# The last output tile in three column parts, and the third w1 chunk in one load

## The chip, the cores and the metric

The kernel runs on one core of one Trainium2 chip. The metric is the device time in microseconds (us), as a median over runs. One profiled run of a kernel also leaves a trace; the span of a trace, from the first to the last instruction, is about 1.7 us shorter than the run's device time. For a program on one core a run counts as fast unless it is over 1.5% above the fastest run of the same kernel. The profile of the kernel before was taken in a throttled execution.

## The reference

Two branches on x (2048 rows, 512 columns, bf16) are mixed by a gate:

```python
g = sigmoid((x * gate_w).sum(-1, keepdims=True))
a = linear_attention(x, wqkv) @ wo         # 32 heads of 16, phi(t) = where(t>0, t+1, exp(t)) + 1e-6
h = layernorm(x)
u = gelu(einsum("bsd,sf->bdf", h, w1) + b1)                     # token MLP, F = 1792
b = (einsum("bdf,fs->bds", u, w2) + b2).transpose(0, 2, 1)
return g * a + (1 - g) * b
```

The change touches how w1 (2048 x 1792) is loaded and how the last 128 of the 2048 output rows are finished.

## The kernel before

w1 comes in four chunks: three of 512 columns (2 MB each) and one of 256 (1 MB). Chunks 0 to 2 are loaded in two halves, the last in one load. All are issued by SyncE's queue without waiting for a buffer, since there are four buffers.

```python
    for c, (j0, nb) in enumerate(w1_chunks):
        w = wpool.tile([P, NT, FB * P], BF16, name="w1c", tag="wc")
        w1c.append(w)
        for t0 in range(0, NT, 8) if c < 3 else (0,):
            t1 = t0 + 8 if c < 3 else NT
            nc.sync.dma_start(
                out=w[:, t0:t1, : nb * P], in_=w1_view[:, t0:t1, j0 * P : (j0 + nb) * P]
            )
        # ... after chunk 0: the loads of wv and wo
```

The output is made in 16 row tiles of 128 rows. Each takes 4 matmuls for the attention branch (`aps`) and 14 for the MLP (`yps`). VectorE mixes both into `ot` (the eviction), and a store follows. The last tile is already split: 384 columns with a store, then 128 columns with a store, so that the eviction of the wide piece runs behind the matmuls of the narrow one.

```python
    for t in range(NT):
        # ... aps: 4 matmuls of 512 columns; ScalarE makes a_sc from it
        for c0, W in ((0, D - P), (D - P, P)) if t == NT - 1 else ((0, D),):
            cs = slice(c0, c0 + W)
            yps = bank("yps")
            for f in range(NF):
                mm(yps[:, :W], w2c[c][:, f, tl * P : (tl + 1) * P], uT[:, f, cs], f == 0, f == NF - 1)
            ot = opool.tile([P, D], BF16, name="ot", tag="ot")
            nc.vector.scalar_tensor_tensor(
                out=ot[:, :W], in0=yps[:, :W], scalar=c1[:, t : t + 1], in1=a_sc[:, cs],
                op0=ALU.mult, op1=ALU.add,
            )
            (nc.scalar if t < 2 else nc.sync).dma_start(out=o_view[:, t, cs], in_=ot[:, :W])
        # ...
```

One thing is not in this source: the framework under it gives every transfer on the hardware queues one of eight completion counters (semaphore lanes), in rotation: the issues count on 100, 103, 104, 105, 106, 108, 109 and 110 in turn. In the instruction listing the loads of x and w1 wait for the transfer eight before them, on the same counter.

## Time and profile before

| | kernel before |
|---|---|
| time, median of the first 3 runs | 163.35 us (163.27 to 163.65) |
| profiled run | 281.43 us, span 279.7 us, granted TensorE clock 0.565: throttled |
| PE busy | 99% of the span |
| one late row tile, throttled | 6.94 us for 18 matmuls of 512 columns |

The first fence is from the page of the kernel before: busy time of each engine, the rows for granted clock and DMA in 40 slices of the span (tenths, then GB/s), and the chain of work that ended last.

```profile
span 279.7 us, 2222 instructions
...
PE 275.8 (99%) x826; PEld 97.0 (35%) x826; DVE 128.3 (46%) x273; ACT 73.8 (26%) x114; POOL 7.2 (3%) x17
...
PEclk9555555555555555555555555555555555555555
DMA  7999995000000008003400707000000000000000
GB/s 196 238 293 352 349 345 145 0 0 0 2 1 0 0 0 265 0 0 104 158 4 0 262 12 251 19 20 23 23 26 20 20 19 19 21 19 19 19 19 19
...
PE 97%; DMA 1%; SPq 0%; DVE 0%; issue 0%
...
```

PE is never free: the chain is 97% PE. The clock row reads 5 (tenths) nearly everywhere, so every PE duration here must be scaled before it says anything about the timed runs (386 ns per matmul of 512 columns here). DMA is busy in the first seven slices, then only in bursts for w2 and lightly for the stores.

The second fence is the timeline of the last tile (start, duration, engine, line, operation, count; in brackets the idle time before it and what ended it).

```profile
...
start us, us, engine line op out<-in xcount [idle before <-releaser]
...
271.45 5.51 PE L110 MATMUL yps<-uT,w2c 128*128 128x384 bf16 x28
...
275.48 1.21 PEld L110 LDWEIGHTS <-w2c 128*128 128x128 bf16 x13 [0.15 <-issue]
275.73 0.62 DVE L500 SCALAR_TENSOR_TENSOR ot<-yps,c,a_sc 128x384 bf16<-128x384 f32 x1 [4.79 <-PE yps L110]
276.99 0.35 DVE L500 SCALAR_TENSOR_TENSOR ot<-yps,c,a_sc 128x128 bf16<-128x128 f32 x1 [0.64 <-PE yps L110]
```

The 28 matmuls of both pieces are merged into one row. The 384-column eviction is done (275.73 + 0.62 us) before the last matmuls end, so the last eviction (276.99) waits for PE alone. The thirteen last weight loads take 1.21 us, 93 ns each: about the pace of 128 columns at this clock (386/4 = 96 ns). The w1 loads are seven issues, the last begun at 34.5 us:

```profile
...
L173 SPq DMA_DIRECT2D w1c<-in_B_w_dram x7: 507/2914/4284, 16.8 to 34.5; - x7
...
```

### The profile page before, as it was taken

The numbers are of one execution on the slowest core, as the hardware profiler recorded it, in microseconds if no ns is written. First come the engines' busy times: TensorE is split into PE (matmuls) and PEld (weight loads), VectorE is DVE, ScalarE is ACT, GpSimd is POOL, SyncE is SP. The second block draws the span as 40 slices with busy tenths as digits, with TensorE's granted clock in tenths as the row PEclk, the third lists the DMA queues.
The fourth block names the chain that finished last, engine by engine and source line by source line (L and its number), as shares of the span: only waits on it lengthen the run. The fifth ranks groups of instructions, "written<-read, shape, count | busy, mean of one in ns | idle before, by whom it ended". The sixth has DMA issues, their size and how long they took to land.

```text
span 279.7 us, 2222 instructions
## 1 busy us (share of the span) xinstructions
PE 275.8 (99%) x826; PEld 97.0 (35%) x826; DVE 128.3 (46%) x273; ACT 73.8 (26%) x114; POOL 7.2 (3%) x17
## 2 busy tenths in 40 slices
PE   8999999999999999999999999999999999999996
PEld 3333333333333333333333333333333333333333
DVE  1835566256465571256597701565555553111111
ACT  3411344124434160235511211222222221111110
POOL 1000310010100000000000000000000000000000
PEclk9555555555555555555555555555555555555555
DMA  7999995000000008003400707000000000000000
GB/s 196 238 293 352 349 345 145 0 0 0 2 1 0 0 0 265 0 0 104 158 4 0 262 12 251 19 20 23 23 26 20 20 19 19 21 19 19 19 19 19
DMA packets 29241, 22.94 MB, mean 82 GB/s; under 512 B 7696, under 2 KB 29200, under 8 KB 29232
## 3 DMA queue, kind: packets, MB, share of 16 engines
q1 hardware_dynamic: 28288, 21.89, 26.2%
q10 hardware_dynamic: 832, 0.79, 0.8%
q0 software_dynamic: 112, 0.14, 0.2%
q8 instruction: 6, 0.10, 0.1%
q14 instruction: 3, 0.02, 0.0%
HBM read 19.01 MB, written 2.10 MB: 75 GB/s over the span
## 4 chain that ended last, share of the span: by engine, by line
PE 97%; DMA 1%; SPq 0%; DVE 0%; issue 0%
PE uacc L110 31%; PE yps L110 31%; PE kacc L110 9%; PE aps L110 9%; PE qacc L110 9%; PE gacc L110 9%; DMA xs<-in_A_x_dram 1%; PE pt L110 0%; PE kvps L110 0%; PE w2ps L110 0%; SPq L126 0%; DVE ot L500 0%; PE pt L327 0%
## 5 line engine op out<-in xcount | busy, mean ns | idle before, releaser
L110 PE MATMUL uacc<-hs,w1c 128*128 128x512 bf16 (+1 forms) x233 | 89.6, 581 | 0.0
L110 PE MATMUL yps<-uT,w2c 128*128 128x512 bf16 (+2 forms) x238 | 89.3, 560 | 0.0
L110 PEld LDWEIGHTS <-w2c 128*128 128x128 bf16 x238 | 31.2, 133 | 55.5 <-issue 55.4
L110 PEld LDWEIGHTS <-w1c 128*128 128x128 bf16 (+1 forms) x233 | 29.4, 131 | 55.3 <-issue 55.2
L500 DVE SCALAR_TENSOR_TENSOR ot<-yps,c,a_sc 128x512 bf16<-128x512 f32 (+2 forms) x17 | 12.2, 719 | 68.6 <-PE yps L110 68.6
L487 ACT ACTIVATE a_sc<-aps,c,gg 128x512 f32<-128x512 f32 x16 | 12.4, 775 | 76.0 <-PE aps L110 76.0
L110 PE MATMUL aps<-W2sb,pqT 128*128 128x512 bf16 x64 | 27.8, 582 | 0.0
L110 PE MATMUL qacc<-xT,wq_sb 128*128 128x512 bf16 x64 | 27.7, 581 | 0.0
L110 PE MATMUL kacc<-wk_sb,xT 128*128 128x512 bf16 x64 | 27.4, 589 | 0.0
L110 PE MATMUL gacc<-pk,xs 128*128 128x512 bf16 x64 | 26.8, 579 | 0.0
L211 DVE TENSOR_SCALAR e<-e 128x512 bf16<-128x512 bf16 x32 | 9.4, 293 | 34.2 <-ACT e L210 34.2
L321 ACT ACTIVATE uT<-uacc,bcol 128x512 bf16<-128x512 f32 x14 | 9.4, 686 | 46.8 <-PE uacc L110 46.8
L386 DVE STREAM_TRANSPOSE zT<-pz 128x512 f32<-128x512 f32 x16 | 11.3, 706 | 18.3 <-ACT pz L385 18.3
L210 ACT ACTIVATE e<-qacc 128x512 bf16<-128x512 f32 x16 | 9.6, 597 | 27.6 <-PE qacc L110 27.6
L210 ACT ACTIVATE e<-kacc 128x512 bf16<-128x512 f32 x16 | 9.6, 597 | 26.7 <-PE kacc L110 26.7
L110 PEld LDWEIGHTS <-xs 128*128 128x128 bf16 x76 | 9.8, 133 | 17.8 <-issue 16.3
L385 ACT ACTIVATE pz<-pqT,zcol 128x512 f32<-128x512 bf16 x16 | 11.4, 714 | 11.5 <-DVE ot L500 11.4
L110 PEld LDWEIGHTS <-wq_sb 128*128 128x128 bf16 x64 | 8.6, 135 | 16.0 <-issue 16.0
L110 PEld LDWEIGHTS <-pqT 128*128 128x128 bf16 x64 | 8.4, 132 | 16.0 <-issue 16.0
L110 PEld LDWEIGHTS <-xT 128*128 128x128 bf16 x64 | 8.2, 130 | 15.3 <-issue 14.7
L250 ACT ACTIVATE hs<-xs,nmr,rstd 128x512 bf16<-128x512 bf16 x16 | 12.7, 802 | 0.0
L395 DVE STREAM_TRANSPOSE rex<-rd 128x512 bf16<-128x512 bf16 x16 | 11.4, 711 | 0.6
(59 smaller groups left out, 116.3 us busy)
## 6 DMA issues: line engine op xcount, KB each, us to landing
w1c<-in_B_w_dram SPq DMA_DIRECT2D x7, 1024.0 KB, 12.4
w2c<-in_B_w_dram SPq DMA_DIRECT2D x8, 896.0 KB, 5.7
out_dram<-ot SPq DMA_DIRECT2D x13, 128.0 KB, 1.7
xs<-in_A_x_dram SPq DMA_DIRECT2D x3, 512.0 KB, 4.4
xs<-in_A_x_dram SPq DMA_DIRECT2D x4, 128.0 KB, 3.3
wk_sb<-in_A_wqkv_dram ACTq DMA_DIRECT2D x2, 256.0 KB, 3.3
wq_sb<-in_A_wqkv_dram SPq DMA_DIRECT2D x1, 512.0 KB, 4.8
wv_sb<-in_A_wqkv_dram SPq DMA_DIRECT2D x1, 512.0 KB, 10.0
```

The lines of the kernel that those rows point to most:

```text
L110: nc.tensor.matmul(o, lhsT=lhsT, rhs=rhs, start=start, stop=stop, **kw)
L210: nc.scalar.activation(out=e[:], in_=acc[:], func=ACT.Exp)
L211: nc.vector.tensor_scalar(out=e[:], in0=e[:], scalar1=1.0, scalar2=PHI_EPS, op0=ALU.min, op1=ALU.add)
L250: nc.scalar.activation(out=hs[:, t, :], in_=xs[:, t, :], func=ACT.Identity, scale=rstd[:, t : t + 1], bias=nmr[:, t : t + 1],)
L321: nc.scalar.activation(out=uT[:, j, :], in_=acc[:], func=ACT.Gelu_apprx_tanh, bias=bcol[:, j : j + 1])
L385: nc.scalar.activation(out=pz[:], in_=seg, func=ACT.Copy, scale=zcol[:, j : j + 1])
L386: nc.vector.transpose(out=zT[:], in_=pz[:])
L395: nc.vector.transpose(out=rex[:].rearrange("p (a d) -> p a d", d=HEAD), in_=rd[:].unsqueeze(2).to_broadcast([P, SC // HEAD, HEAD]),)
L487: nc.scalar.activation(out=a_sc[:], in_=aps[:], func=ACT.Identity, scale=gg[:, t : t + 1], bias=c2[:, t : t + 1],)
L500: nc.vector.scalar_tensor_tensor(out=ot[:, :W], in0=yps[:, :W], scalar=c1[:, t : t + 1], in1=a_sc[:, cs], op0=ALU.mult, op1=ALU.add,)
```

## The change

The last tile in three parts of 256, 128 and 128 columns, and the third w1 chunk in one load. The apparent intent is to have less work left when the matmuls end, and one transfer less.

```diff
-        for t0 in range(0, NT, 8) if c < 3 else (0,):
-            t1 = t0 + 8 if c < 3 else NT
+        for t0 in range(0, NT, 8) if c < 2 else (0,):
+            t1 = t0 + 8 if c < 2 else NT
...
-        for c0, W in ((0, D - P), (D - P, P)) if t == NT - 1 else ((0, D),):
+        for c0, W in ((0, 2 * P), (2 * P, P), (3 * P, P)) if t == NT - 1 else ((0, D),):
```

## The prediction

> **What bounds the kernel.** The page shows PE busy 99% of the span, and the chain of waits is 97% PE matmuls; DMA is 1% of it. The profile fell in a throttled execution: span 279.7 us at a granted clock of 0.565, while the timed runs took 163.35 us, so I scale it. In the timeline a late row tile (4 aps and 14 yps matmuls of 512 columns) takes 6.94 us, 386 ns per matmul. [...] with 6.9 us of start, 2.7 us of tail, and 1.7 us by which the profiled run's time exceeds its span, 162.3 us. About 1 us is left for stalls of fast runs alone. So fast runs too are bound by matmul columns.
>
> **The w1 load.** One 2 MB load replaces two of 1 MB. In the profile all w1 transfers are issued by 37.7 us, and the DMA row is empty after the seventh slice (49 us). [...] Chunk 0, needed first, lies ahead in the same queue and isn't touched. One load less shifts the semaphore lanes of later transfers and gives w2 loads waits on lanes long done. Worth on the critical path: 0.0 us.
>
> **The last tile.** Before: 14 matmuls of 384 columns, then 14 of 128. After: 256, 128, 128. PE columns are equal; 14 weight loads and matmuls are added. In the trace the last 13 weight loads run 93 ns apart, which is 128 columns at 0.57 of full clock: narrow matmuls still pay only for columns. [...] The last piece stays 128 columns: its eviction (0.35 us) and store (1.4 us to landing) are unchanged.
>
> Was the last piece held up by the 384 piece? At full clock (T = end of the 384 matmuls): eviction T+0.05 to 0.67, store issue 0.70 to 1.03 (0.62 and 0.33 us in the trace); the last matmul ends at T+0.78, its eviction runs to 1.15, its store issues at 1.20. Neither DVE nor the queue is late, by 0.1 to 0.2 us. The split relieves only a near miss: the store ahead of the last one shrinks from 96 to 32 KB and sits 0.78 us, not 0.5 us, ahead. I allow 0 to 0.15 us for less overlap of the transfers. Net: -0.05 us, +-0.1.
>
> **Prediction.** 163.3 us, range 162.9 to 163.75. Faster by over 2%: 1%; within 2%: 97%; slower by over 2%: 2%.
>
> **What would show it.** At equal clock: 840 instead of 826 PE matmuls; the PE stretches before the last tile unchanged; no PE wait on w1c; 18 evictions at the output line, 17 before; the last eviction starting within 0.05 us of the last matmul, the last store landing in 1.4 us. The stretch from the last aps matmul to the end within 0.2 us of before.
>
> **What would make it wrong.** A throttled state in the timed runs (the profile shows that it exists), narrow matmuls bound at full clock by weight load (over 60 ns each), the middle store's issue delaying the last, or a stall in fast runs at w1 that the throttled profile hides and that the shifted lanes move.

In the first paragraph the sum of 162.3 us has lost the PE stretch scaled to full clock, 151 us. It can be had from what was measured afterwards: in the trace of the changed kernel 15 late row tiles, 270 matmuls, take 58.275 us, 215.8 ns each, and 270.1 x 215.8/386 = 151 us. In the second an estimate of when chunk 2 is first read is cut; measured, it is 31.8 us after the chunk landed. In the third a fixed cost for the 14 added matmuls is cut, 0.035 us; with it and the middle of the allowance for less overlap (0.075 us) the net came to about -0.05 us. Measured, those matmuls cost 0.035 us as well (62.174 against 62.139 us, in the table below). The T+0.78 us is an estimate that stays: the trace of the changed kernel has its last 128-column matmuls 56 ns apart, and 14 of them are 0.78 us.

## The result and the profile after

| | before | after |
|---|---|---|
| time, median of 6 runs of the same rounds | 163.31 us (163.14 to 163.65) | 163.14 us (162.93 to 163.90) |
| ratio, fast runs | | 0.9995, 95% interval 0.9971 to 1.0019 |
| profiled run | 279.7 us at clock 0.565 | 161.4 us at clock 0.998 |
| matmuls | 826 | 840 |

A ratio is the mean time of one kernel's fast runs over that of the other's in the same rounds, so it is not quite the ratio of the medians. Not even the sign is resolved.

The profile after fell in a full-clock execution. This is its page:

```profile
span 161.4 us, 2253 instructions
...
PE 157.3 (97%) x840; PEld 72.5 (45%) x840; DVE 124.6 (77%) x274; ACT 72.9 (45%) x114; POOL 7.3 (5%) x17
...
PEclk9999999999999999999999999999999999999999
DMA  4999999999930006700940588501000001110001
GB/s 162 227 235 262 292 360 318 363 347 348 319 93 0 0 0 213 246 0 0 318 141 2 172 283 262 192 33 37 33 33 33 33 33 48 54 65 33 33 33 33
...
PE 95%; DMA 3%; SPq 1%; DVE 0%; issue 0%
...
```

PE has 118.5 us less busy time than before, which is the clock and not the change: the kernel before at full clock (e1) has 157.1 us. The DMA row now fills the first eleven slices (44 us), about the same time as before. The chain is 95% PE, 3% the first loads of x. The timeline of the last tile and the chain of waits over the last two tiles:

```profile
...
start us, us, engine line op out<-in xcount [idle before <-releaser]
...
155.13 3.29 PEld L110 LDWEIGHTS <-w2c 128*128 128x128 bf16 x42
155.35 3.25 PE L110 MATMUL yps<-uT,w2c 128*128 128x256 bf16 x42
155.52 3.83 SPq L504 DMA_DIRECT2D out_dram<-ot  x4
...
157.13 0.48 DVE L500 SCALAR_TENSOR_TENSOR ot<-yps,c,a_sc 128x256 bf16<-128x256 f32 x1 [1.64 <-PE yps L110]
157.86 0.35 DVE L500 SCALAR_TENSOR_TENSOR ot<-yps,c,a_sc 128x128 bf16<-128x128 f32 x1 [0.24 <-PE yps L110]
158.64 0.35 DVE L500 SCALAR_TENSOR_TENSOR ot<-yps,c,a_sc 128x128 bf16<-128x128 f32 x1 [0.43 <-PE yps L110]
```

```profile
...
151.62 3.02 PE yps L110 x14
154.65 0.86 PE aps L110 x4
155.51 3.11 PE yps L110 x42
158.62 0.02 issue
158.64 0.35 DVE ot L500
```

There are three evictions, each finished before the next begins. The last starts 0.02 us after the last matmul. At full clock 14 matmuls of 512 columns take 3.02 us (216 ns each).

These two traces can't be compared for a change of 0.1 us, because their clocks differ. So the first experiment was the unchanged kernel again, to get its trace at full clock.

### The profile page after: what moved, and what is told of

The parts are those of the page before. It is cut to its first block, busy times and chain, and to the rows that moved or that the text cites. A ratio compares the mean times of both kernels' runs of the same rounds, so it can differ in the third digit from the quotient of the medians.

```text
span 161.4 us, 2253 instructions
## 1 busy us (share of the span) xinstructions
PE 157.3 (97%) x840; PEld 72.5 (45%) x840; DVE 124.6 (77%) x274; ACT 72.9 (45%) x114; POOL 7.3 (5%) x17
## 4 chain that ended last, share of the span: by engine, by line
PE 95%; DMA 3%; SPq 1%; DVE 0%; issue 0%
PE uacc L110 30%; PE yps L110 30%; PE aps L110 9%; PE gacc L110 9%; PE qacc L110 9%; PE kacc L110 8%; DMA xs<-in_A_x_dram 3%; SPq L126 1%; PE kvps L110 0%; PE pt L110 0%; PE w2ps L110 0%; DVE ot L500 0%; PE pt L327 0%
## 5 line engine op out<-in xcount | busy, mean ns | idle before, releaser
L110 PE MATMUL uacc<-hs,w1c 128*128 128x512 bf16 (+1 forms) x233 | 51.5, 379 | 0.0
L110 PE MATMUL yps<-uT,w2c 128*128 128x512 bf16 (+2 forms) x252 | 51.0, 355 | 0.0
L110 PE MATMUL aps<-W2sb,pqT 128*128 128x512 bf16 x64 | 16.4, 379 | 0.0
L110 PE MATMUL qacc<-xT,wq_sb 128*128 128x512 bf16 x64 | 16.4, 379 | 0.0
L110 PE MATMUL kacc<-wk_sb,xT 128*128 128x512 bf16 x64 | 16.1, 379 | 0.1
L110 PE MATMUL gacc<-pk,xs 128*128 128x512 bf16 x64 | 15.8, 379 | 0.0
L214 DVE SCALAR_TENSOR_TENSOR pqT<-qacc,e 128x512 bf16<-128x512 f32 x16 | 11.1, 692 | 0.6
L214 DVE SCALAR_TENSOR_TENSOR pk<-kacc,e 128x512 bf16<-128x512 f32 x16 | 11.1, 692 | 0.6
L388 DVE TENSOR_REDUCE den<-zT 128x32 f32<-128x512 f32 x16 | 11.0, 686 | 0.6
L234 DVE BATCH_NORM_STATS2 stats<-xs 128x6 f32<-128x512 bf16 x16 | 10.9, 683 | 0.0
```

Source lines behind the costliest of these rows:

```text
L110: nc.tensor.matmul(o, lhsT=lhsT, rhs=rhs, start=start, stop=stop, **kw)
L214: nc.vector.scalar_tensor_tensor(out=dst, in0=acc[:], scalar=0.0, in1=e[:], op0=ALU.max, op1=ALU.add)
L234: nc.vector.bn_stats(out=stats[:], in_=xs[:, t, :])
L388: nc.vector.tensor_reduce(out=den[:], in_=zT[:].rearrange("p (a d) -> p a d", d=HEAD), op=ALU.add, axis=AX.X)
```

## The experiments

All twelve runs gave correct results. The edit of each is against the kernel named. The traces turned out to be far finer than the times. From the first `gacc` matmul (9.4 to 10.2 us after the start) to the last matmul nothing moves except by the kernel's own edits, so each trace can be cut into stretches. (`gacc` are the products of x and phi(k), `uacc` those of the token MLP with w1; `aps` and `yps` belong to the row tiles.) Worked out from the start and landing records of each trace, in us:

| run | first gacc | first gacc to first aps | first aps to last matmul's start | from there to last landing | last landing to end | sum against e1 | measured: difference of medians |
|---|---|---|---|---|---|---|---|
| e1 before, again | 9.63 | 86.61 | 62.139 | 2.101 | 0.914 | 0 | +0.10 |
| changed kernel, first trace | 9.60 | 86.61 | 62.174 | 2.094 | 0.913 | +0.03 | -0.17 |
| e4 changed, again | 9.37 | 86.60 | 62.174 | 2.095 | 0.904 | +0.02 | -0.05 |
| e2 tail only | 9.71 | 86.61 | 62.175 | 2.076 | 1.191 | +0.29 | +0.36 |
| e3 w1 only | 9.76 | 86.61 | 62.139 | 2.108 | 0.965 | +0.06 | +0.54 |
| e12 w1 only, again | 9.72 | 86.60 | 62.139 | 2.112 | 0.969 | +0.06 | +0.38 |
| e11 lane only | 9.74 | 86.60 | 62.139 | 2.123 | 1.196 | +0.30 | +0.53 |
| e5 one piece | 9.48 | 86.61 | 61.944 | 2.955 | 1.025 | +0.77 | +1.13 |
| e6 halves | 9.82 | 86.61 | 62.086 | 2.359 | 0.960 | +0.25 | +0.39 |
| e8 last 64 | 9.58 | 86.61 | 62.234 | 2.145 | 1.405 | +0.63 | +0.71 |
| e7 thin all | 9.42 | 86.61 | 65.717 | 2.080 | 1.024 | +3.67 | +3.56 |
| e9 w1 all one | 9.85 | 86.61 | 62.174 | 2.112 | 1.019 | +0.15 | +0.30 |
| e10 w1 late | 10.17 | 86.61 | 62.174 | 2.094 | 0.914 | +0.03 | -0.09 |

"Sum against e1" adds the four stretches after the first gacc matmul. The start is left out, since it scatters by 0.8 us between single executions and its loads are the same in all.

### e1: the kernel before, again

Edit: none.

> The kernel before, unchanged: a null run and, if its profile falls in an untrottled execution, the first trace of it at full clock. Theory (nothing on the chain changed): ratio 1.000 within its interval; the last 128-column piece ends about 0.8 us after the 384-column piece, its eviction starts within 0.05 us of the last matmul, and the time from the last matmul to the end of the span is 2.7 to 2.8 us, as in the throttled trace (2.73) and in the changed kernel (2.78). Rival (a near miss was relieved by the change): here the last eviction waits for the 384-column eviction, or the last store lands 0.1 us or more later than in the changed kernel.

Measured: 163.21 us, ratio 1.0011 (0.9995 to 1.0028). The chain of waits at its end:

```profile
...
155.54 3.07 PE yps L110 x28
158.61 0.03 issue
158.64 0.35 DVE ot L500
```

The timeline of the same trace has both evictions of the last tile in one row:

```profile
...
157.91 1.08 DVE L500 SCALAR_TENSOR_TENSOR ot<-yps,c,a_sc 128x384 bf16<-128x384 f32 x2 [2.39 <-PE yps L110]
```

The 384-column eviction is done at 158.53 us (157.91 + 0.62, its duration in the throttled trace), before the last matmul ends (158.61). The last eviction starts 0.03 us after the last matmul and does not wait for it. The last store lands 2.101 us after the last matmul's start against 2.094 us in the changed kernel. So there was no near miss to relieve: the two transfers' overlap was worth 0.007 us, not up to 0.15 us, and even that is less than this stretch scatters between traces with the same tail (2.101 to 2.123 us with two pieces). The rival falls. The profile was at full clock, which makes this the trace of before for all that follows.

### e2, e3, e4: each half alone, and both

Edit of e2: the tail's line of the change alone. Edit of e3: the two w1 lines of the change alone. e4 is the changed kernel.

> Only the three-part tail, w1 as before. Theory: both parts are worth nothing, ratio 1.000, tail as in the changed kernel (3.1 us of last-tile yps matmuls, 0.35 us eviction, 2.8 us from last matmul to the end). Rival (the parts cancel: one gains some tenths, the other loses as much): this run differs from before by over 0.3 us, with the w1-only run as far off on the other side.

> Only the one 2 MB load of the third w1 chunk, tail as before. Theory: ratio 1.000, PE never waits for w1c, PE stretch from the first uacc matmul to the first aps matmul equal within 0.1 us (63.3 us in the changed kernel). Rival (the parts cancel): over 0.3 us off, with the sign opposite to the tail-only run.

> The changed kernel again on the same chip as the three others. Theory: ratio 1.000, interval within 0.3%. Rival: the sum of the tail-only and the w1-only differences, if either is not nil.

| | median us | ratio | 95% interval |
|---|---|---|---|
| e2 tail only | 163.47 (163.37 to 163.56) | 1.0021 | 1.0009 to 1.0033 |
| e3 w1 only | 163.65 (163.41 to 165.67) | 1.0052 | 1.0016 to 1.0089 |
| e4 both | 163.06 (162.88 to 163.62) | 1.0005 | 0.9989 to 1.0020 |

My theory (both parts worth nothing) missed: each half alone was slower, and together they were not. My rival missed too, for the halves do not have opposite signs. So the halves interact. The trace of e2 shows where: matmuls as in the changed kernel to 0.001 us, the last landing no later, but 1.191 us in place of 0.913 us from the last landing to the end of the span. The waits of SyncE after its last store are all at one line of the kernel's end. The instructions of that line in e1 (first fence) and in e2 (second), with shortest, median and longest duration in ns:

```profile
...
L532 SPq EVENT_SEMAPHORE  x9: 17/28/28, 159.4 to 161.3; - x9
...
```

```profile
...
L532 SPq EVENT_SEMAPHORE  x9: 17/28/1030, 159.5 to 161.7; - x9
...
```

One of the nine waits lasts 1030 ns in e2 and none does in e1. The single records behind these rows, from the two traces (start in us, ns, the counters it asks for):

```
e1 (before)                                e2 (tail only)
last store counts on 110                   last store counts on 100
159.409   17  103                          159.506   17  103
159.462   28  104, 100                     159.560 1030  104, 100   <- last store lands 160.567
159.524   28  105, 113                     160.624   28  105, 113
159.588   28  106, 112                     160.688   28  106, 112
159.649   28  108, 111                     160.750   28  108, 111
160.191   27  109, 102  <- 109: 160.174    160.809   28  109, 102
160.497   28  110, 107  <- 110: 160.480    160.871   28  110, 107
160.562  drain                             160.936  drain
161.394  end of span                       161.758  end of span
```

At its end the program asks all completion counters, one after the other, in a fixed order, about 62 ns each. In e1 the last store counts on counter 110, which is asked last, so everything else has been asked by the time it lands. (The last store of e1 shows 16 increments, from 160.314 to 160.480 us, and the question for it ends after the sixteenth.) In e2 there is one transfer more, the rotation moves on by one, and the last store counts on counter 100, which is in the second question. The five questions left (0.3 us) come after the landing. (Where a wait shows depends on the question: in e2 the landing of the second-named counter, 100, is waited for inside the 1030 ns, while in e1 the waits for 109 and 110, named first, are gaps ahead of questions of 27 and 28 ns.) The changed kernel has one store more and one load less. Its last store is back on 110, and its end takes 0.913 us as before.

The e3 kernel has one transfer less, so its last store counts on 109, asked one before the last: 0.965 us, 0.05 us more. That does not explain e3's half microsecond. (One run of e3, 165.67 us, lifts its ratio: it is 1.4% above the kernel's fastest and so still counts as fast. Without it the ratio is 1.003, still above 1. The median hardly moves.)

This is the theory from here on: the two halves of the change are tied to each other by the rotation of the counters.

### e5, e6, e8: other last pieces

Edits against the changed kernel (e5: one piece; e6: two of 256; e8: 256, 128, 64, 64):

```diff
-        for c0, W in ((0, 2 * P), (2 * P, P), (3 * P, P)) if t == NT - 1 else ((0, D),):
+        for c0, W in ((0, D),):                                                                    # e5
+        for c0, W in ((0, 2 * P), (2 * P, 2 * P)) if t == NT - 1 else ((0, D),):                   # e6
+        for c0, W in ((0, 2 * P), (2 * P, P), (3 * P, P // 2), (3 * P + P // 2, P // 2)) if t == NT - 1 else ((0, D),):  # e8
```

> The last tile in one piece of 512 columns with one store, w1 as in the change. Theory (what counts is only the eviction of the last piece, and pieces before it are hidden): the last eviction is 0.75 us in place of 0.35 and the last store is 128 KB (1.7 us to landing in place of 1.4 to 1.5), so 0.6 to 0.7 us longer from the last matmul to the end, 0.07 us less on PE; time +0.4 to +0.7 us, ratio about 1.003 to 1.004. Rival (the tail is fixed by the end of the program and not by the last piece): tail as in the change, ratio 1.000.

> Last tile in two pieces of 256. Theory: last eviction 0.48 us, last store 64 KB (1.5 us), so 0.13 to 0.2 us longer from the last matmul to the end than in the change, 0.035 us less on PE; ratio about 1.001, not resolved by time, to be read from the profile. Rival (number of pieces matters, not the last width): equal to or shorter than before.

> Last tile in pieces of 256, 128, 64 and 64. Theory: last eviction about 0.28 us (from 0.35 at 128, 0.48 at 256), last store 16 KB about 1.4 us, so at most 0.1 us gained from the last matmul on, if the 14 weight loads of 64-column matmuls stay hidden [...] about 0.05 to 0.1 us lost on PE; net within 0.1 us. Rival (narrower is better all the way): 0.1 us or more shorter in the profile.

Measured: e5 164.21 us, ratio 1.0075 (1.0055 to 1.0095); e6 163.47 us, 1.0023 (1.0005 to 1.0040); e8 163.79 us, 1.0048 (1.0028 to 1.0068). The PE times came as expected: the last tile's yps matmuls take 3.04 us in e5 and 3.07 us in e6 against 3.11 us in the changed kernel, and the last matmul of e8 starts 0.060 us later (62.234 against 62.174 us). The chain of waits at the end of e5:

```profile
...
155.39 3.04 PE yps L110 x14
...
158.51 0.75 DVE ot L500
```

e5: the last eviction takes 0.75 us and the 128 KB store lands later. From the end of the last matmul (158.43 us) to the end of the span (162.01 us) it is 3.58 us, against 2.78 us in e1 (158.61 to 161.39 us). Of these 0.80 us, 0.11 us is the counter (108, asked two before the last). So in the trace splitting the last tile at all is worth some 0.7 us, as expected; it is the next split that has nothing left to gain. The time missed its expectation (+0.4 to +0.7 us): it is +1.13 us. e6 has the 0.48 us eviction that was expected, and 0.05 us at the counter. e8's last eviction is 0.28 us, as expected. But its last store lands 2.145 us after the last matmul's start, no sooner than with 128 columns, and with one transfer more its last store is on counter 100 again. Its 64-column matmuls follow one another every 29 ns, against 56 ns with 128 columns, so no weight load held them up. Its end took another 0.2 us in the final handshake of the engines, in this one trace: SyncE's last drain starts at 161.636 us, those of PE, VectorE and ScalarE by 161.315 us. I have no cause for that part. The expectation "net within 0.1 us" missed: the sum is 0.60 us over the changed kernel's, of which 0.49 us is the end. A narrower last piece gains nothing here.

All three lie further from before in time than their traces say, by 0.08 to 0.36 us. For e5 and e6 the record shows where: outside the span. The device time exceeds the span by 1.70 to 1.72 us on average in the runs of before, but by 2.05 us in e5 and 1.83 us in e6. The same holds for e9 (1.88 us), e3 (1.80) and e12 (1.78). These five are the kernels with fewer transfers than before; in all others it is 1.68 to 1.75 us. Why, no experiment shows.

### e7: all tiles in three pieces

```diff
-        for c0, W in ((0, 2 * P), (2 * P, P), (3 * P, P)) if t == NT - 1 else ((0, D),):
+        for c0, W in ((0, 2 * P), (2 * P, P), (3 * P, P)):
```

> All 16 row tiles in pieces of 256, 128 and 128, so that the cost of the 28 more matmuls of a tile is taken 15 times over (420 matmuls; against before's two-piece last tile 434 more). Theory (only a fixed cost per matmul): 2.5 ns each, +1.05 us, ratio about 1.0065; a tile goes from 3.89 to 3.96 us. Rival A (narrow matmuls bound by the weight load at full clock, 60 ns or more each): +4 ns or more for each of 450 narrow matmuls on top, +2 us or more. Rival B (three stores a tile stall the queue or DVE): PE waits for a yps bank, tiles uneven.

The traces had shown the 2.5 ns by then: 0.035 us for 14 more matmuls (62.174 against 62.139 us). The changed kernel's last 128-column matmuls are 56 ns apart, so rival A's 60 ns would be 4 ns more.

Measured: 166.64 us, ratio 1.0217 (1.0196 to 1.0238; verdict "unclear", as the interval reaches over the 2% line), three times what the fixed cost alone would give. The chain of waits shows two regimes. In the late tiles (first fence) a tile's yps matmuls take 3.09 us; in the early ones (second fence) PE drops off the chain:

```profile
...
138.23 0.86 PE aps L110 x4
139.09 3.09 PE yps L110 x42
142.19 0.22 PE aps L110
142.40 0.05 issue
142.45 0.59 PE aps L110 x2
143.05 3.09 PE yps L110 x42
...
```

```profile
...
111.31 0.73 ACT pz L385
112.06 0.72 DVE zT L386
112.81 0.70 DVE den L388
113.53 0.36 DVE rd L393
113.91 0.72 DVE rex L395
...
115.00 0.51 DVE ot L500 x2
115.51 3.18 DMA out_dram<-ot
...
```

In the late tiles 42 matmuls take 3.09 us where 14 took 3.02 us: 0.07/28 = 2.5 ns for each additional matmul, the expected fixed cost. It repeats from tile to tile, so narrow matmuls are not bound by weight loads (rival A falls). Over 15 tiles that is 1.05 us of the 3.54 us by which the stretch from the first aps grew. The other 2.5 us came in the early tiles, where VectorE also normalizes the attention (`den`, `rex`), and where the chain runs through VectorE, ScalarE and a wait of 3.18 us for a store to land, so that a pool buffer comes free. That is rival B, and it holds for these tiles. Nothing of this bears on the last tile, where VectorE and the buffers are free (in the changed kernel VectorE idles 0.43 us before the last eviction, which starts 0.02 us after the last matmul).

### e9, e10: the w1 loads

Edit of e9 against the changed kernel: every w1 chunk in one load.

```diff
-        for t0 in range(0, NT, 8) if c < 2 else (0,):
-            t1 = t0 + 8 if c < 2 else NT
+        for t0 in range(0, NT, 8) if c < 0 else (0,):
+            t1 = t0 + 8 if c < 0 else NT
```

Edit of e10 against the changed kernel: chunk 2 is left out of the loop and loaded after the third gelu, behind a small write into its tile that the load overwrites.

```diff
+        if c == 2:
+            continue
...
+    nc.scalar.activation(out=w1c[2][:, 0, 0:8], in_=uT[:, NB0 - 1, 0:8], func=ACT.Copy)
+    nc.sync.dma_start(out=w1c[2][:], in_=w1_view[:, :, 8 * P : 12 * P])
```

> Every w1 chunk in one 2 MB load (the last in its one 1 MB load as before), tail as in the change. Theory (split is of no use wherever the whole chunk has landed before its first matmul): chunks 1 and 2 worth nothing; chunk 0 is first read at 32.9 us in the changed kernel's trace, its halves were issued from 16.8 to 18.7 us and landed 8.5 to 15 us later, so it's a near thing, 0 to 1 us lost and none if it lands before 32.9. Rival (fewer transfers save issue time or lanes and so bring data earlier): faster by 0.3 us or more.

> The third w1 chunk's one load is held back until the third gelu of chunk 0 has run (a small write into its tile, which the load then overwrites), so that it starts near 59 to 60 us instead of near 28 us. First reader near 75 us. Theory (over 20 us of slack): it lands near 66 to 68 us, PE doesn't wait, ratio 1.000. Rival (the load was near the critical path, so that its form could matter): PE waits for w1c, over 0.3 us longer.

Measured: e9 163.52 us, ratio 1.0023 (1.0003 to 1.0043); e10 163.13 us, ratio 0.9998 (0.9978 to 1.0017). What touched the tile w1c in the changed kernel, in e9 and in e10 (durations of issues, then what its readers' engine waited for in us):

```profile
...
L173 SPq DMA_DIRECT2D w1c<-in_B_w_dram x6: 507/2142/5887, 16.8 to 31.6; - x6
...
  issue: 0.2, 1
...
```

```profile
...
L173 SPq DMA_DIRECT2D w1c<-in_B_w_dram x4: 507/3706/6430, 16.8 to 32.4; - x4
...
  issue: 0.2, 1
...
```

```profile
...
L422 SPq DMA_DIRECT2D w1c<-in_B_w_dram x1: 368/368/368, 61.9 to 61.9; - x1
...
  issue: 0.2, 1
...
  ACT uT L323: 17.2, 8
...
```

No PE wait for a w1 load is to be seen in any of the three; the 0.2 us is issue. In the changed kernel chunk 2 lands at 43.73 us and is first read at 75.49 us, so there are 31.8 us of slack. In e10 it is issued at 61.93 us, lands at 71.5 us and is read at 76.06 us, and nothing is lost (63.30 us from the first uacc matmul to the first aps matmul in all). In e9 the whole of chunk 0 lands at 29.27 us, 3.9 us before its first reader at 33.16 us. e9's matmul stretches are those of the changed kernel. What its trace has more is 0.11 us at the end: two transfers less, so the last store is on counter 108, asked two before the last. e10 has as many transfers as before, its counter is 110, its end 0.914 us. The rivals fall. In these traces the form of the load shows only as a count; the times of the w1-only kernel (e3, e12) leave a part open.

### e11, e12: the count alone, and w1 only once more

e11 is the kernel before with its last w1 load split in two. PE, VectorE, ScalarE and GpSimd run the same instructions in the same order as before.

```diff
-        for t0 in range(0, NT, 8) if c < 3 else (0,):
-            t1 = t0 + 8 if c < 3 else NT
+        for t0 in range(0, NT, 8):
+            t1 = t0 + 8
```

> The kernel before with its last w1 load split in two, and nothing else: PE, DVE, ACT and POOL programs are the same as before; one transfer more, so the last store counts on completion counter 100, which the final sequence of waits asks second, in place of 110, which it asks last. Lane theory (formed from the ends of the traces so far: 0.91 us from the last landing to the end of the span when the last store's counter is asked last, 0.96 one earlier, 1.02 two earlier, 1.19 when asked second): 1.19 us from landing to end, matmul stretch of the last rows as before (62.14 us from the first aps to the last matmul), so +0.28 us and ratio about 1.0017, like the tail-only run, though the tail has two pieces. Rival (the third piece is what made the tail-only run slower): end 0.91 us after landing, ratio 1.000.

> The w1-only kernel a second time. Its first run was 0.5% (0.5 us) slower, of which the end of its trace shows only 0.05 to 0.06 us (counter asked one before the last), and all stretches between the first gacc matmul and the last matmul are equal to before. Lane theory: the rest was scatter of the start, so this time +0.06 us, ratio 1.000 to 1.001. Rival (one load of 2 MB costs something that profiles don't show): again +0.4 us or more.

Measured: e11 163.54 us, ratio 1.0030 (1.0014 to 1.0045); e12 163.39 us, ratio 1.0021 (1.0001 to 1.0041). The waits at the end of e11:

```profile
...
L532 SPq EVENT_SEMAPHORE  x9: 17/28/1057, 159.5 to 161.7; - x9
...
```

Here too one wait lasts over a microsecond, the one that asks for counter 100. The end takes 1.196 us after the landing, as the counter theory said to 0.01 us, with the two-piece tail of before. So the loss of 0.28 us in e2's trace is not from the third piece of the tile. A transfer more, here among the loads of w1, does it. Over all traces the end takes 0.90 to 0.91 us after the last landing when the last store's counter is asked last, 0.96 to 0.97 us one earlier, 1.02 us two earlier, and 1.19 to 1.20 us when it is asked second (1.41 us once, in e8). The time is +0.53 us where the trace says +0.30 us; the interval reaches down to +0.23 us.

e12's trace repeats e3's to 0.005 us in every stretch after the start, and again its time is higher (0.38 us) than the 0.06 us that its trace explains. So in both, twelve runs in all, the w1-only kernel was slower by 0.3 to 0.5 us than the stretches account for. By the medians my expectation of +0.06 us missed, and the rival's +0.4 us came near; but e12's interval (1.0001 to 1.0041) still reaches down to +0.06 us, while e3's does not. No stretch after the first gacc matmul holds the difference, and the rival's cause, the single load, is in the changed kernel and in e10 too, where nothing is lost. Of the excess, 0.06 to 0.10 us lies outside the span (see e5). The rest, some 0.3 to 0.4 us, may lie in the start, which scatters, or in something that the profiled executions did not have; e1, an exact copy, was also off by 0.10 us, and e11, with two loads for that chunk, by 0.23 us. I could not settle it.

## Why the prediction was right

The number (163.3 us, measured 163.14 us) held. Step by step:

- **PE-bound, and by columns.** Right. At full clock the chain is 95% PE, a late row tile takes 3.89 us (0.86 + 3.02 and rounding), 18 times 215.8 ns. The "1 us left for stalls of fast runs" was not stalls: from the first gacc matmul on the chain has no wait worth naming. A part of it is work that did not scale with the clock, such as the 64 small kv matmuls, which take 0.59 us in both traces (clock 0.565 and 0.998) and which I had scaled down (0.26 us). Another part is the 386 ns, which was a little high: the 15 row tiles from 166.26 to 270.10 us of the throttled trace took 6.92 us each, 384.6 ns per matmul, which makes the estimate 0.5 us longer. Together this is the size of the gap; that it is the whole of it is not shown.
- **Fourteen more matmuls.** The forecast's term was 0.035 us, and the traces give 62.174 against 62.139 us. e7 confirms 2.5 ns each.
- **The last eviction and store don't depend on the piece ahead.** Right: e1 shows the last eviction 0.03 us after the last matmul. The allowance of 0 to 0.15 us for less overlap measured 0.007 us, so the net of matmuls and tail was +0.03 us, not -0.05 us. That is inside the +-0.1 us allowed, but the overlap term was mis-sized and with it the sign of the net, far below what the times resolve.
- **"Worth on the critical path: 0.0 us" for the w1 load.** Right for the data: 31.8 us of slack in the trace, and e10 used up over 27 us of it for nothing. But I had the counters in view ("One load less shifts the semaphore lanes of later transfers") and looked only at whether earlier waits would block. I did not ask which counter the last store would land on. The tail's third store alone costs 0.28 us at the end of the program (e2), the merged load alone costs 0.05 us there (e3), and both together put the last store back on the counter that is asked last. The zero was the outcome of two shifts that I had not seen; that they undid each other was luck.
- **What would have made it wrong** did not occur: all timed runs were fast, the last 128-column matmuls ran 56 ns apart in the trace after, at 2.5 ns for each one added, the middle store did not delay the last, and PE did not wait for w1.

So the change moved the time by nothing because the tail was already hidden behind PE (the part before the last piece) or unchanged (the last piece), and because its one side effect cancelled within the change. The traces put it at +0.02 to +0.03 us from the first gacc matmul on. What stays open is most of the 0.3 to 0.5 us by which the w1-only kernel ran slower than its trace says, and why kernels with fewer transfers spend 0.06 to 0.34 us more outside the span.

## What to carry to other kernels

Here, with a last piece of 128 columns, splitting the pieces ahead of it further bought nothing (+0.02 to +0.03 us in the traces): look for whether the last eviction starts right at the last matmul, and stop there. A change in the number of transfers can move the end of a program by some tenths of a microsecond (0.28 us in e2 and e11), though no transfer lies on the critical path, if the program asks its completion counters in a fixed order. So test two halves of a change apart, and where times scatter by 0.3 us, cut traces into stretches between fixed events, and compare those.
